# A first transpose copy moved from ScalarE to VectorE, and a pair's queries placed ahead of an exponential

## The chip, the cores and the metric

The kernel runs on one core of one Trainium2 chip. The core has five engines that run their own instruction streams and meet at semaphores: TensorE (PE, matmuls and transposes into PSUM), VectorE (DVE), ScalarE (ACT), GpSimd (POOL) and SyncE (SP). The metric is the device time of one execution in microseconds. A profile's span runs from the first to the last instruction, and the execution's own time is a little longer.

## The reference

Attention that selects chunks of keys, followed by a feed-forward network. Shapes: 4 batches, 8 heads, 768 tokens, 64 elements per head; the feed-forward goes from 512 to 2048 and back.

```python
k_min, k_max = min and max of k over chunks of 32 keys
ub = sum(maximum(q * k_min, q * k_max), axis=-1)      # one bound per query and chunk
ub = where(causal, ub, -1e9)
top_chunks = argsort(ub)[..., -6:]                    # six chunks per query
scores = where(selected & causal, q @ k.T / 8, -1e9)
attn = softmax(scores)
x = (attn @ v), heads side by side                    # 3072 x 512
h = maximum(x @ w_in, 0)
out = (h * h) @ w_out
```

## The kernel before

**Tiling.** A slot is one pair of heads in one half (384 tokens) of one batch. There are 32 slots, four to a half. `ORDER` gives the halves; slots 0 to 3 are the first half of batch 0, slots 4 to 7 the first half of batch 1. In the code a slot is `s`, `NP` is 4, and the fifth and sixth pairs are slots 4 (`s == NP`) and 5 (`s + 1`). All of it lies in one program without loops on the chip: the Python loops write the instruction order out by hand, and each engine works through its own list in that order.

**Steps of a slot.** `step_T` (L274) transposes keys and queries on PE into two PSUM tiles, `tk` and `tq`. `relus_T` (L295) makes ReLU of the queries and of their negatives on ACT (`qr`), which the bounds need. `extrema` (L237, L240) reduces the keys to minima and maxima per chunk on DVE (`km`, `kbd`). `place` (L300) copies transposed keys or queries, one head at a time, into the tile `kq` that the score matmuls read. `step_U` (L378 to L398) computes the bounds `ub` on PE, the sixth largest by MAX8 on DVE, and writes `chosen`. `step_V` transposes `chosen` on PE (`qt`, L442) and copies it on DVE under the queries in `kq` (L447), two copies. `step_E` (L460, L471) does the score matmuls of one head into a PSUM bank `ps` and the exponential on ACT into `e`. `step_F` (L493 to L503) multiplies with the values into `po`; DVE takes a reciprocal `r` and writes the normalised `x`.

**From x to the feed-forward.** For the first half, x is transposed on PE: `x_T` (L531) for slots 0 and 1 together into one PSUM tile `pt`, and again for slots 2 and 3. `x_copy` (L537) copies each `pt` into `xT`, 128 x 768 each. `push` then queues the feed-forward's blocks. `ffn_up` (L579) makes 128 of the 2048 inner columns with four matmuls, one for each head pair of `xT`, into `ph`; ACT applies the ReLU and DVE squares it. The first two blocks go straight to `h` (L585) and are squared later (L586); most others go over `ht` (L589, L590). `ffn_down` (L602) multiplies with `w_out`.

**PSUM tiles that are shared.** The pool `psF` has two banks under the tag `ph`. They are used in turn by `tk` of the early slots, the two `pt` tiles, and the `ph` blocks. The pool `psY` has one bank, which holds `tq` of the early slots one after the other: the sixth pair's `tq` waits until the fifth pair's queries have been placed.

**The order around the change.** Slot 3 is the last turn of the first loop. Its last turn does the exponentials of slot 3, `x_T(0, 0, F)`, its copy on ACT, the placing of the fifth pair's queries and of one head of its keys on ACT, `step_F(3)`, and `step_V(4)`. The next loop starts with slot 4: `step_P(5)` (the transposes of the sixth pair), `x_T(0, 1, F)` with its copy on DVE, `relus_T(5)`, the first exponential of slot 4 (`step_E(4, 0, 0)`), `push(0)`, and then `extrema(5)` and the placing of the sixth pair. The instructions of `push` are given out later by `f1()`, one block at a time.

**Loads.** POOL issues the loads of k, q, v and of both weights from lists by slot (`later`); `w_in` comes in three pieces (L631), `w_out` in two (L636). SP issues DMA transposes and the output. An issue on POOL waits until the one that used its semaphore eight issues before has landed.

Of the kernel before, what the change touches and what calls it, by code (L numbers as in the profile page):

```python
# [39 lines left out]
def kernel(  # L40
# [9 lines left out]
    nc = tc.nc  # L50
# [178 lines left out]
    def extrema(s, part=None):  # L229
        b, half, p = slots[s]  # L230
        kv = st[s]["k"].rearrange("r (j c e) -> r c j e", j=TP, c=12)
        if part in (None, 0):
            st[s]["km"] = work.tile([128, 2, 12], BF16, tag="km", name="km")
        km = st[s]["km"]
        for w in range(2):
            if part in (None, w):
                nc.vector.tensor_reduce(km[:, w, :], kv, axis=AX.XY, op=(ALU.min, ALU.max)[w])  # L237
        if part in (0, 1):
            return
        nc.vector.tensor_mul(  # L240
            kbds[b % 2][:, p, :, :, 12 * half:12 * half + 12], hmask,
            km.unsqueeze(2).to_broadcast([128, 2, 2, 12]))

    def in_order(x):

        return x.rearrange("r (j p) -> r p j", j=TP)

    def by_token(x):
        return x.rearrange("r (p j) -> r p j", j=TP)
# [36 lines left out]
    def relus_T(s):  # L286
        b, half, p = slots[s]
        t = st[s]
        qr = t["qr"] = work.tile([128, 2, HB], BF16, tag="qr", bufs=3, name="qr")
        c = 128 * (1 - half)  # L290
        for w in range(2):
            o, i = qr[:, w, c:], t["q"][:, c:]
            if s >= NP:
                o, i = by_token(o), in_order(t["q"])[:, c // TP:, :]
            nc.scalar.activation(o, i, ACT.Relu, scale=(-1.0, 1.0)[w])  # L295

    def place(s, n, copy, h0=0, h1=2):
        b, half, p = slots[s]
        for h in range(h0, h1):
            copy(by_token(kqs[b % 2][0:D, p, 2 * half + "kq".index(n), h, :]),  # L300
                 in_order(st[s][n][D * h:D * h + D]))
# [216 lines left out]
    def xT_of(hb):  # L518
        if hb not in xTs:
            xTs[hb] = late.tile([128, NKI, HB], BF16, tag="xT", name="xT")  # L520
        return xTs[hb]
# [14 lines left out]
    def x_copy(hb, g, u0, u1, copy):  # L536
        copy(xT_of(hb)[:, 2 * g + u0:2 * g + u1, :], pts[hb, g][:, u0:u1, :])  # L537
# [143 lines left out]
    def busy(n, pool=psA, tag="att"):  # L681

        idle = pool.tile([128, 128], F32, tag=tag, name="idle")
        for _ in range(n):
            nc.tensor.matmul(idle, lhsT=ident, rhs=ident, start=True, stop=True)  # L685
# [33 lines left out]
    for s in range(NP):  # L719
        last = s + 1 == NP  # L720
        if s:
            step_E(s, 0, 0)
            if not last:

                step_T(s + 2, F, Y, "k")
                extrema(s + 2, 0)
            step_E(s, 0, 1)
        if last:
            step_F(s - 1, 0)
            step_F(s - 1, 1)  # L730
        step_E(s, 1, 0)
        step_U(s + 1)
        if not last:
            busy(3)
            extrema(s + 2, 1)
            place(s + 1, "k", nc.scalar.copy)
        step_E(s, 1, 1)
        if last:
            x_T(0, 0, F)
            x_copy(0, 0, 0, 2, nc.scalar.copy)  # L740
            place(s + 1, "q", nc.scalar.copy)
            place(s + 1, "k", nc.scalar.copy, 1, 2)
            step_F(s, 0)
            step_F(s, 1)
            step_V(s + 1)
        else:
            step_T(s + 2, F, Y, "q")
            relus_T(s + 2)
            step_V(s + 1)
            if s:  # L750
                step_F(s - 1, 0)
                step_F(s - 1, 1)
            extrema(s + 2, 2)
            if s + 2 == NP:
                place(s + 2, "k", nc.vector.tensor_copy, 0, 1)
        go(s, 99)
# [6 lines left out]
    for s, (b, half, p) in enumerate(slots):  # L763
        if s < NP:
            continue
        hb = s // NP
        nb = len(BANKS[half])
        hf = nb // 2
        quota = [((5, 5, 4, 4) if hb == 1 else (8, 5, 6, 7) if hb == 2 else (8, 6, 7, 7))[p]]
        for fn, *a in first.get(s, ()):  # L770
            fn(*a)
        if (hb == ON_PE - 1 and p == 2) or (ON_PE < hb < 2 * B - 1 and p == 0):
            parts.extend(step_K(hb + 1))

        def f1():
            if quota[0] and queue:
                quota[0] -= 1
                fill(1, True)

        if s == NP:  # L780
            step_P(s + 1)
            x_T(0, 1, F)
            x_copy(0, 1, 0, 2, nc.vector.tensor_copy)
            relus_T(s + 1)
            for n in range(hf):
                step_E(s, 0, n)
            push(0)
            extrema(s + 1)
            place(s + 1, "k", nc.vector.tensor_copy)
            place(s + 1, "q", nc.scalar.copy)  # L790
        if s == 2 * NP:
            for n in range(hf):
                step_E(s, 0, n)
            relus_T(s + 1)
            place(s + 1, "q", nc.scalar.copy)
            step_F(s - 1, 0)
            step_F(s - 1, 1)
            f1()
            x_T(1, 1, F, (1,))
            f1()  # L800
            extrema(s + 1)
            place(s + 1, "k", nc.vector.tensor_copy)
            put_off()
            x_copy(1, 1, 1, 2, nc.vector.tensor_copy)
            push(1)
        if p == 0 and hb > 2:
            step_F(s - 1, 0)
            step_F(s - 1, 1)
            put_off()
            push(hb - 1)  # L810
        else:
            f1()
        if s > NP and s != 2 * NP:
            for n in range(hf):
                step_E(s, 0, n)
        k1()
        f1()
        if p == 0 and hb > 2:
            f1()
            f1()  # L820
        if hb > 1 and s != 2 * NP:
            f1()
        if hb < ON_PE:
            go(s, 4 if s == 2 * NP else 2)
        for n in range(hf, nb):
            step_E(s, 0, n)
        if hb < ON_PE and p:
            k1()
        if s + 1 == ON_PE * NP:
            f1()  # L830
        if s < NS - 2 or s + 1 == 3 * NP:
            step_U(s + (1 if hb < ON_PE else 2))
        if s == NP:
            put_off()
        if s + 1 == ON_PE * NP:
            put_off(2)
        if hb >= ON_PE and s < NS - 2:
            step_W(s + 2)
        if s == 2 * NP:

            for x in nsel:
                nc.vector.memset(
                    x[:, :, :, :, 1, :].rearrange("p i h j c -> p (i h j) c"), 0.0)
        late_f = half == 0 and hb > 2
        border = p == 0 and hb > 1
        if not border and not (late_f and p == NP - 1) and s + 1 not in (2 * NP, 3 * NP):
            f1()
        if p and s > NP:
            step_F(s - 1, 0)
            step_F(s - 1, 1)  # L850
        for fn, *a in by_sp.get(s, ()):
            fn(*a)
        if s + 1 == ON_PE * NP:
            step_P(s + 2)
            step_Q(s + 2)
        if half == 0 and not (late_f and p in (0, NP - 1)):
            f1()
        if hb < ON_PE and p:
            k1()
        for n in range(hf):  # L860
            step_E(s, 1, n)
            if border and half and n == 0:

                f1()
        if not (late_f and p == 0):
            f1()
        if s + 1 <= ON_PE * NP:
            step_V(s + 1)
        if s + 1 == ON_PE * NP:
            put_off(2)  # L870
        if hb == ON_PE and p == 0:
            parts.extend(step_K(hb + 1))
        k1()
        if hb < ON_PE:
            go(s, 99)
        for n in range(hf, nb):
            step_E(s, 1, n)
        if hb >= ON_PE:
            go(s, 99)
        k1()  # L880
        if hb == ON_PE - 1 or (hb == ON_PE and p):
            k1()
        if s + 1 < ON_PE * NP:
            step_P(s + 2)
            if s + 2 == ON_PE * NP:
                step_Q(s + 2)
        if s + 1 == ON_PE * NP:
            f1()
            step_U(s + 2)
            step_W(s + 2)  # L890
        if hb >= ON_PE or s + 1 == ON_PE * NP:
            if s + 3 < NS:
                step_P(s + 3)
                step_Q(s + 3)
        f1()
        if half == 0:
            f1()
        while quota[0] and queue:
            f1()
# [40 lines left out]
```

## Time and profile before

| | |
|---|---|
| median of 3 runs | 265.12 us (264.89 to 265.48) |
| profiled execution, its own time | 265.17 us |
| its span | 263.5 us |
| granted TensorE clock | 1.00 |
| PE busy | 253.6 us (96%) |
| ACT busy | 178.4 us (68%) |
| DVE busy | 162.9 us (62%) |
| POOL busy | 91.0 us (35%) |

A row of a timeline gives the start, the time it took, the engine, the line, the operation, and out<-in with shapes; "x6" merges six instructions in a row. In brackets stands the idle time of the engine just before, and what ended it. A row of the chain gives start, length and what. PEld is PE's weight load, and L12 is line 12 of the kernel before. Matmul ends are modelled, and successors on ACT and DVE may start a little before their predecessor's recorded end.

### The profile page before, as it was taken

How to read it: one execution, taken by the hardware profiler on the slowest of the kernel's cores; microseconds unless marked ns; L12 is line 12 of the kernel's file. 1: busy time of each engine (PE TensorE's matmuls, PEld its weight loads, DVE VectorE, ACT ScalarE, POOL GpSimd, SP SyncE). 2: the span in 40 equal slices, each digit the busy share in tenths (PEclk: the TensorE clock that was granted, in tenths of full speed). 3: DMA queues.
4: the chain of work that ended last, by engine and by line, in shares of the span. 5: the costliest groups of instructions: out<-in, count | busy, mean ns of one | idle time of the engine just before them, and what ended most of it. 6: DMA issues, size and time to landing. Idle time of an engine off the chain costs nothing.

```text
span 263.5 us, 6549 instructions
## 1 busy us (share of the span) xinstructions
PE 253.6 (96%) x2398; PEld 157.4 (60%) x2424; DVE 162.9 (62%) x619; ACT 178.4 (68%) x399; POOL 91.0 (35%) x134
## 2 busy tenths in 40 slices
PE   7898899999999999999999999999999999999995
PEld 6576565556676566655565566745565665645543
DVE  6788998867995568566875566554863233424411
ACT  4899997698984787944785778835685788614500
POOL 8957445607911444225520552310221111000000
PEclk9999999999999999999999999999999999999999
DMA  7999999999994999999995999995642220111022
GB/s 138 166 188 188 207 219 183 131 196 137 135 154 96 138 163 165 142 152 150 189 133 138 142 145 145 166 165 131 112 110 62 67 45 17 56 42 41 0 82 80
DMA packets 116162, 33.69 MB, mean 128 GB/s; under 512 B 102561, under 2 KB 112577, under 8 KB 116129
## 3 DMA queue, kind: packets, MB, share of 16 engines
q0 software_dynamic: 65200, 13.83, 64.0%
q1 hardware_dynamic: 49984, 19.03, 38.2%
q10 hardware_dynamic: 944, 0.39, 0.6%
q8 instruction: 19, 0.31, 0.5%
q14 instruction: 15, 0.11, 0.2%
HBM read 27.26 MB, written 6.29 MB: 127 GB/s over the span
## 4 chain that ended last, share of the span: by engine, by line
PE 88%; ACT 5%; DVE 4%; issue 2%; POOL 0%; ACTq 0%; POOLq 0%
PE ph L579 29%; PE py L602 29%; PE ps L460 13%; PE po L493 8%; ACT e L471 2%; PE ub L382 2%; PE idle L685 2%; PE py L567 1%; PE tk L274 1%; ACT kq L300 1%; DVE km L343 1%; PE qt L431 1%; DVE km L237 1%; PE qt L442 1%; ACT qr L295 1%
## 5 line engine op out<-in xcount | busy, mean ns | idle before, releaser
L471 ACT ACTIVATE e<-ps 128x512 bf16<-128x512 f32 x192 | 96.8, 550 | 18.6 <-PE ps L460 16.9
L579 PE MATMUL ph<-xT,w_in 128*128 128x384 bf16 x512 | 98.9, 325 | 0.7 <-ACT h L585 0.5
L602 PE MATMUL py<-w_out,h 128*128 128x512 bf16 x342 | 82.7, 379 | 1.9 <-issue 0.3
L590 DVE TENSOR_TENSOR h<-ht 128x384 bf16<-128x384 bf16 x114 | 41.8, 376 | 55.4 <-ACT ht L589 54.9
L475 POOL TENSOR_SCALAR_AFFINE_SELECT e<-e 128x384 bf16<-128x384 bf16 x56 | 30.1, 537 | 127.6 <-ACT e L471 127.5
L589 ACT ACTIVATE ht<-ph 128x384 bf16<-128x384 f32 x114 | 55.5, 500 | 26.9 <-PE ph L579 26.5
L579 PEld LDWEIGHTS <-w_in 128*128 128x128 bf16 x512 | 47.9, 97 | 31.4 <-issue 2.1
L460 PE MATMUL ps<-kq 96*128 96x384 bf16 (+2 forms) x320 | 58.0, 278 | 1.4 <-DVE kq L436 1.2
L602 PEld LDWEIGHTS <-h 128*128 128x128 bf16 x368 | 34.7, 97 | 35.3 <-issue 0.6
L460 PEld LDWEIGHTS <-kq 96*128 96x128 bf16 x320 | 26.4, 97 | 16.1 <-issue 1.7
L493 PEld LDWEIGHTS <-e 128*128 128x128 bf16 x672 | 25.2, 98 | 3.9
L493 PE MATMUL po<-vn,e 128*128 128x65 bf16 x672 | 26.8, 194 | 0.0
L396 DVE MAX8 m<-ub 128x8 f32<-128x16 f32 (+4 forms) x160 | 16.2, 168 | 15.7 <-PE ub L389 9.3
L608 ACT COPY ob<-py 128x512 f32<-128x512 f32 x18 | 10.6, 586 | 22.6 <-PE py L602 22.3
L503 DVE TENSOR_TENSOR x<-po,r 128x384 bf16<-128x384 f32 x32 | 17.8, 558 | 1.1
L109 POOL DMA_DIRECT2D kn<-in_k_dram x15 | 13.4, 897 | 0.4 <-issue 0.3
L237 DVE TENSOR_REDUCE km<-tk 128x12 bf16<-128x384 bf16 x24 | 12.5, 551 | 1.5 <-PE tk L274 1.2
L109 POOL DMA_DIRECT2D qn<-in_q_dram x15 | 13.3, 895 | 0.2
L125 POOL DMA_DIRECT2D vn<-in_v_dram x15 | 12.5, 842 | 2.3 <-DMA qn<-in_q_dram 1.5
L343 DVE TENSOR_TENSOR km<-km 128x384 bf16<-128x384 bf16 (+3 forms) x40 | 12.0, 300 | 1.1
L382 PEld LDWEIGHTS <-qr 128*128 128x128 bf16 x160 | 7.8, 96 | 4.1 <-DVE qr L323 1.0
L382 PE MATMUL ub<-kbd,qr 128*128 128x48 bf16 (+1 forms) x160 | 9.6, 180 | 0.6 <-DVE kbd L240 0.3
(79 smaller groups left out, 193.3 us busy)
## 6 DMA issues: line engine op xcount, KB each, us to landing
out_dram<-ob SPq DMA_DIRECT2D x23, 256.0 KB, 2.5
w_out<-in_moe_w_out_dram POOLq DMA_DIRECT2D x2, 1024.0 KB, 18.0
kn<-in_k_dram POOLq DMA_DIRECT2D x15, 128.0 KB, 6.0
qn<-in_q_dram POOLq DMA_DIRECT2D x15, 128.0 KB, 5.8
kq<-kqT SPq DMA_DIRECT2D x10, 192.0 KB, 4.7
vn<-in_v_dram POOLq DMA_DIRECT2D x4, 384.0 KB, 8.1
vn<-in_v_dram POOLq DMA_DIRECT2D x9, 128.0 KB, 8.0
w_in<-in_moe_w_in_dram POOLq DMA_DIRECT2D x2, 512.0 KB, 9.2
```

Of the source, the lines that this page charges most:

```text
L109: nc.gpsimd.dma_start(out=nat_of(n, g)[:, DM * j:DM * j + DM].rearrange("p (h d) -> p h d", d=D), in_=rows(n, *ORDER[g], 0, H)[:, 128 * j: ...
L382: nc.tensor.matmul(ub[:, j - j0], lhsT=st[s]["qr"][:, w, 128 * j:128 * (j + 1)], rhs=kbds[b % 2][:, p, w, :, 0:ncs], start=bool(half) and ...
L396: nc.vector.max(out=m8[:, j, hh, :], in_=ub[:, j - j0, hh, 0:12 * half + 4 * j + 4])
L460: nc.tensor.matmul(ps[:, at:at + 128 * m], lhsT=kqs[b % 2][0:KR, p, 2 * (j // HT), hh, 128 * (j % HT):128 * (j % HT + 1)], rhs=qc(s, hh)[: ...
L471: nc.scalar.activation(e[:, 512 * n + lo:512 * n + hi], ps[:, lo:hi], ACT.Exp, scale=float(scale))
L475: nc.gpsimd.affine_select(out=d, in_=d, compare_op=ALU.is_ge, fill=0.0, base=0, channel_multiplier=-1, pattern=[[0, 3], [1, 128]])
L493: nc.tensor.matmul(po[:, hh, i, :], lhsT=t["e"][hh][:, c:c + 128], rhs=vn[b % 2][:, 2 * p + hh, j, :], start=(j == 0), stop=(j == iq))
L503: nc.vector.tensor_mul(x[:, p].rearrange("p j (h d) -> p h j d", h=2), po[:, :, :, 0:D], r.to_broadcast([128, 2, HT, D]))
L579: nc.tensor.matmul(ph[:, 0:HB], lhsT=w_in[:, ki, 128 * f:128 * (f + 1)], rhs=xT[:, ki, :], start=(ki == 0), stop=(ki == NKI - 1))
L589: nc.scalar.activation(ht, ph[:, 0:HB], ACT.Relu)
L590: nc.vector.tensor_mul(h, ht, ht)
L602: nc.tensor.matmul(py[t], lhsT=h2[hb, f][:, 128 * t:128 * (t + 1)], rhs=w_out[:, f, :], start=(f == 0), stop=(f == NFI - 1))
```

## The change

Two lines. The copy of the first `pt` (slots 0 and 1) into `xT` is written by `nc.vector.tensor_copy` instead of `nc.scalar.copy`. It keeps its place in the program: on DVE it stands between the selection (`chosen`) of the fifth pair and the reciprocal of slot 3. And the placing of the sixth pair's queries (two copies on ACT) is called ahead of `step_E(4, 0, 0)` instead of behind the placing of its keys. On ACT these copies then stand between the ReLUs of the sixth pair and the fifth pair's first exponential. The orders of PE, POOL and SP are the same as before.

```diff
@@ -737,7 +737,7 @@
         step_E(s, 1, 1)
         if last:
             x_T(0, 0, F)
-            x_copy(0, 0, 0, 2, nc.scalar.copy)
+            x_copy(0, 0, 0, 2, nc.vector.tensor_copy)
             place(s + 1, "q", nc.scalar.copy)
             place(s + 1, "k", nc.scalar.copy, 1, 2)
             step_F(s, 0)
@@ -782,12 +782,12 @@
             x_T(0, 1, F)
             x_copy(0, 1, 0, 2, nc.vector.tensor_copy)
             relus_T(s + 1)
+            place(s + 1, "q", nc.scalar.copy)
             for n in range(hf):
                 step_E(s, 0, n)
             push(0)
             extrema(s + 1)
             place(s + 1, "k", nc.vector.tensor_copy)
-            place(s + 1, "q", nc.scalar.copy)
```

## The prediction

> **What bounds the kernel now.** I read the page's head and chain first, then the busy time by stage, then the chain and the rows of each engine around 20 to 30 us, where the changed lines run.
>
> ```profile
> span 263.5 us, 6549 instructions
> PE 253.6 (96%) x2398; PEld 157.4 (60%) x2424; DVE 162.9 (62%) x619; ACT 178.4 (68%) x399; POOL 91.0 (35%) x134
> PE 88%; ACT 5%; DVE 4%; issue 2%; POOL 0%; ACTq 0%; POOLq 0%
> ```
>
> TensorE (PE) is the bound over the whole span: busy 253.6 of 263.5 us, and 88% of the chain that ended last. The next rows give busy time in stretches of the span (length, then busy time and count of each engine, then clock, DMA share and GB/s).
>
> ```profile
> 24.00:28.00 4.00, 3.31 (x29) 2.06 (x26) 3.53 (x12) 3.35 (x9) 2.21 (x4) 1.00 1.47 202
> ...
> 30.00:38.00 8.00, 7.68 (x85) 4.91 (x81) 7.63 (x26) 7.32 (x20) 4.13 (x7) 1.00 1.28 215
> ...
> 60.00:120.00 60.00, 59.38 (x613) 37.73 (x617) 43.32 (x173) 43.99 (x97) 25.95 (x35) 1.00 1.33 145
> 120.00:180.00 60.00, 59.38 (x525) 36.21 (x531) 36.23 (x149) 40.39 (x88) 21.41 (x30) 1.00 1.31 149
> ```
>
> From 60 to 180 us PE has about 1% idle, at a granted clock of 1.00, so a lead won before that should last. In 24 to 28 us PE is busy only 3.31 of 4 us. There the chain (start, length, what) runs through ScalarE (ACT):
>
> ```profile
> 21.89 0.69 ACT xT L537
> ...
> 23.88 0.66 ACT qr L295 x2
> ...
> 24.56 0.35 issue
> 24.91 0.60 ACT e L471
> ...
> 26.38 0.50 ACT h L585
> ...
> 26.92 1.46 PE ph L579 x8
> ...
> 30.20 0.28 DVE kq L447
> ```
>
> The reader is to see that the copy to be moved stands in this chain, that 0.35 us ahead of the fifth pair's first exponential have no cause the profile names, and that the next feed-forward matmuls start 0.04 us behind the first ReLU (26.38 + 0.50).
>
> **The change part by part.** First the copy of x's first two transposes. ACT's own rows:
>
> ```profile
> 21.77 0.81 ACT L537 COPY xT<-pt 128x768 bf16<-128x768 bf16 x1
> 22.45 0.97 ACT L300 COPY kq<-tq 64x384 bf16<-64x384 bf16 x2
> 23.32 0.47 ACT L300 COPY kq<-tk 64x384 bf16<-64x384 bf16 x1
> ...
> 25.41 0.95 ACT L300 COPY kq<-tq 64x384 bf16<-64x384 bf16 x2
> ```
>
> ACT loses one instruction, and the fifth pair's query copies start at 21.77 instead of 22.45: 0.68 us earlier. What waits for them on PE:
>
> ```profile
> 21.05 0.50 PE L531 MATMUL pt<-ident,x 128*128 128x128 bf16 x6
> ...
> 23.47 0.37 PE L274 MATMUL tq<-ident,qn 96*64 96x96 bf16 x8 [0.80 <-ACT kq L300]
> 23.77 0.51 PE L531 MATMUL pt<-ident,x 128*128 128x128 bf16 x6
> 24.12 0.38 PE L460 MATMUL ps<-kq 96*128 96x384 bf16 x2
> ...
> 24.99 1.14 PE L579 MATMUL ph<-xT,w_in 128*128 128x384 bf16 x6 [0.16 <-DVE xT L537]
> ...
> 26.14 0.25 PE L382 MATMUL ub<-kbd,qr 128*128 128x24 bf16 x4
> 26.92 1.30 PE L579 MATMUL ph<-xT,w_in 128*128 128x384 bf16 x7 [0.53 <-ACT h L585]
> ```
>
> The sixth pair's query transposes (tq) share one bank with the fifth pair's and sat 0.80 us on those copies. They move from 23.47 to 22.79, and ACT's two ReLUs behind them (qr) from 23.88 to 23.20, ending 23.86: 0.68 us of the chain.
>
> VectorE (DVE) gains one instruction. Its rows:
>
> ```profile
> 21.77 0.21 DVE L398 TENSOR_TENSOR chosen<-ub,m 128x48 bf16<-128x48 f32 x1
> 22.28 0.20 DVE L502 RECIPROCAL r<-po 128x6 f32<-128x6 f32 x1 [0.30 <-PE po L493]
> 22.51 0.56 DVE L503 TENSOR_TENSOR x<-po,r 128x384 bf16<-128x384 f32 x1
> 23.10 0.60 DVE L447 COPY kq<-qt 32x256 bf16<-32x256 bf16 x2
> 24.38 0.56 DVE L537 COPY xT<-pt 128x768 bf16<-128x768 bf16 x1 [0.68 <-ACT qr L295]
> 24.85 1.01 DVE L237 TENSOR_REDUCE km<-tk 128x12 bf16<-128x384 bf16 x2
> ...
> 28.78 0.61 DVE L590 TENSOR_TENSOR h<-ht 128x384 bf16<-128x384 bf16 x2
> 29.81 0.36 DVE L590 TENSOR_TENSOR h<-ht 128x384 bf16<-128x384 bf16 x1 [0.42 <-ACT ht L589]
> ```
>
> The price of the added copy is in the row of its twin, 128x768 at 24.38: 0.56 us, and the next instruction starts 0.47 us after it. Its transposes end at 21.55 (21.05 + 0.50). DVE is free between 21.89 and 21.98 (successors overlap by about 0.1 us), so I put the copy at 21.89 and the reciprocal at 22.36 instead of 22.28. The idle 0.30 us ahead of the reciprocal covers the copy but for 0.08 us; without that cover it would cost 0.47. Queued behind it on DVE are the normalisation of x, then to end at 23.15 instead of 23.07, and the two code copies, at 23.18. The fifth pair's scores and the second set of x's transposes wait for these.
>
> The second set of transposes needs that x, and the tq ahead of it on PE (done 22.79 + 0.30). So it moves from 23.77 to 23.18, not to 23.09: late next is x, by DVE, and the lead there is 0.59 us. The second copy on DVE follows from 24.38 to 23.79, and the feed-forward's wait for it (24.99) to 24.40. The reductions and everything behind them on DVE take the same 0.59; if the copy starts at 21.98, 0.50.
>
> [...]
>
> Second, the order on ACT. The two copies of the sixth pair's queries (0.95 together) now go ahead of the exponential. No instruction is added, no DMA is issued, and PE's, POOL's and SP's orders are unchanged. The copies need only tq, ready since 23.16. They start about 23.76 (an ACT successor starts 0.10 us before its predecessor's recorded end: 24.91 + 0.60 against 25.41) and end at 24.71. The exponential's scores on PE move with x from 24.12 to 23.53 and end by 23.91, so they are there. It starts at 24.61, which is still before 24.91.
>
> What the 0.35 us of unnamed wait does is not shown by the trace. Its bounds are nothing (it was something that now passes under the copies) and 0.35 again (it belongs to this instruction). A cost above 0.35 has no row. I take nothing, because the copies put 0.7 us between the scores' end and the exponential, and I keep 0.35 for the range.
>
> The sum at the first ReLU of the feed-forward: 24.61 + 0.50 = 25.11 instead of 26.38, or 25.46 with the 0.35 us. Its matmuls are done by 24.9 (24.40 + 0.49 for two). It ends at 25.61 and the next matmuls could start at 25.65. PE itself is then just through the bound's matmuls (ub), which wait for DVE: 26.14 - 0.59 = 25.55, plus about 0.15. So they start at 25.70 instead of 26.92, a lead of 1.2 us; with the 0.35 us at 26.00, a lead of 0.9.
>
> Late next is DVE. It runs without a gap from 24.38 to 29.39 and carries 0.59; then comes the idle 0.42 ahead of the product at 29.81, which waited for ACT's ht. ACT and PE are 0.9 to 1.2 us earlier there, so the product can move by 0.59 + 0.42 = 1.01 us. From 30.20, in the stretch 30 to 38, DVE (7.63 of 8) paces the loop and hands its lead on. The lead is then the smaller of DVE's 1.01 and PE's 1.2 (or 0.9): 1.0, or 0.9.
>
> The profiled execution took 265.17 us by its own time, 1.67 more than its span, and 0.05 above the median of 265.12. 265.17 - 1.0 is 264.17, or about 264.15 as a median.
>
> **The rivals.** The lead of 1.0 us must pass the weights that are still loading:
>
> ```profile
> 20.41 0.77 POOL L631 DMA_DIRECT2D w_in<-in_moe_w_in_dram  x1
> ...
> 22.49 0.93 POOL L636 DMA_DIRECT2D w_out<-in_moe_w_out_dram  x1
> ...
> 32.29 0.67 POOL L104 DMA_DIRECT2D qn<-in_q_dram  x1 [0.94 <-DMA w_in<-in_moe_w_in_dram]
> ```
> ```profile
> 33.31 0.81 PE L579 MATMUL ph<-xT,w_in 128*128 128x384 bf16 x4
> ```
>
> *Most of the lead is taken back.* The last half of w_in, issued at 20.41, was in by 32.29, when POOL's wait for it ended. The ninth up-projection block, the first to read it, ran at 33.31 and would now be ready at 32.3. There is no room left: a landing 0.5 us later, or a product wait that doesn't give up its 0.42, leaves 0.5 to 0.6 us of lead, a time of about 264.65. Against it: in this execution the landing still fits, and DVE's loop at 30 to 38 had the block's matmuls well ahead of their use.
>
> *The copy holds up DVE, and the kernel is slower.* POOL writes DMA issues from 20.41 to 23.42 (22.49 + 0.93) without a stop. If DVE's copy can't run beside them, it starts at 23.42 instead of 21.89. Each 0.1 us of delay takes 0.1 from the 0.59, so nothing is left at 22.48; the 0.42 of idle covers to 22.90; from there the kernel is slower. At 23.42 it loses 0.5 us: 265.7. Against it: the normalisation at 22.51 also reads PSUM, ran beside the w_out issue, and took 0.56 us. [...]
>
> *The reorder does nothing by itself.* If PE had been ready later than ACT, placing the queries first would only delay the exponential. The rows say otherwise (0.53 us of PE idle on the ReLU). With the copy's move alone DVE's 0.59 would be the lead, near the first rival's time.
>
> **How the numbers follow.** The forecast (lead 0.9 to 1.0, 264.1 to 264.3) has 0.67. Most of the lead taken back or not used (264.65) has 0.18; the copy held up (265.7) has 0.08. What I have not named has 0.07, spread as 0.03 faster, 0.02 same, 0.02 slower. A measurement of this kernel can tell about 0.2%, 0.53 us, from no change: the runs before spread from 264.89 to 265.48. Faster by more than that is below 264.59: 0.67 + 0.03 = 0.70. Within: 0.18 + 0.02 = 0.20. Slower: 0.08 + 0.02 = 0.10. The range goes from PE's full lead of 1.2 and 0.2 of spread (263.7) to the first rival with 0.36 of spread above it (265.0), which leaves out the held-up copy and part of the unnamed. The signs are not balanced, so there is no second range.
>
> **What would show it.** In the profile after: tq at about 22.8; a DVE copy of xT at 21.9 taking 0.56, with x's last normalisation less than 0.2 us later than before; the exponential behind the query copies at 24.6 without a gap; the feed-forward's third block near 25.7 to 26.0 and PE's 0.53 us of idle gone; the DVE product's 0.42 us of idle gone and the code copies of 30.20 near 29.2. The prediction is wrong if the copy starts after 22.5, if the 0.35 us comes back larger, if PE waits for w_in near 32.3, or if the lead seen at 30 us is not in the span.

## The result, and the profile after

The changed kernel takes 264.07 us (median of 6 runs, 263.95 to 264.68) against 265.31 us before (6 runs, 264.89 to 265.48): a ratio of 0.996, with a 95% interval of 0.9947 to 0.9973. The forecast was 264.15 us, within 263.7 to 265.0.

The profiled execution was the slowest of the six: 264.68 us by its own time. Its page's head and the chain's shares, and then busy time by stage (the stretch and its length, busy time and count of PE, PEld, DVE, ACT and POOL):

```profile
span 263.0 us, 6549 instructions
PE 254.2 (97%) x2398; PEld 157.9 (60%) x2424; DVE 163.2 (62%) x620; ACT 177.7 (68%) x398; POOL 91.0 (35%) x134
...
PE 86%; DVE 8%; ACT 3%; issue 2%; POOL 0%; DVEq 0%; ACTq 0%; POOLq 0%
```
```profile
24.00:28.00 4.00, 3.80 (x30) 2.29 (x29) 3.87 (x14) 3.58 (x9) 2.35 (x4) 1.00 1.43 205
...
30.00:38.00 8.00, 7.68 (x83) 4.95 (x81) 7.68 (x26) 7.43 (x20) 4.09 (x6) 1.00 1.29 214
```

PE is busy 3.80 of 4 us in 24 to 28, where it was 3.31. VectorE's share of the chain has grown from 4% to 8%, ScalarE's fallen from 5% to 3%.

Two profiles of this kernel can't be laid over each other as they are: they start out of step. The second pair's normalisation of x, far ahead of the change, stands at 19.63 us before and at 19.95 after, from DVE's timelines:

```profile
19.63 0.56 DVE L503 TENSOR_TENSOR x<-po,r 128x384 bf16<-128x384 f32 x1
```
```profile
19.95 0.56 DVE L503 TENSOR_TENSOR x<-po,r 128x384 bf16<-128x384 f32 x1
...
22.10 0.21 DVE L398 TENSOR_TENSOR chosen<-ub,m 128x48 bf16<-128x48 f32 x1
22.37 0.56 DVE L537 COPY xT<-pt 128x768 bf16<-128x768 bf16 x1
22.84 0.19 DVE L502 RECIPROCAL r<-po 128x6 f32<-128x6 f32 x1
23.07 0.56 DVE L503 TENSOR_TENSOR x<-po,r 128x384 bf16<-128x384 f32 x1
...
24.28 0.56 DVE L537 COPY xT<-pt 128x768 bf16<-128x768 bf16 x1
24.76 1.01 DVE L237 TENSOR_REDUCE km<-tk 128x12 bf16<-128x384 bf16 x2
25.80 0.18 DVE L240 TENSOR_TENSOR kbd<-hmask,km 128x48 bf16<-128x48 bf16 x1
...
28.45 0.94 DVE L590 TENSOR_TENSOR h<-ht 128x384 bf16<-128x384 bf16 x3
29.43 0.60 DVE L447 COPY kq<-qt 32x256 bf16<-32x256 bf16 x2
```

So every time after is 0.32 us late for reasons that lie ahead of the change, and a lead is counted from that row in each profile. The code copies at 30.20 before stand at 29.43: 0.77 earlier as printed, 1.09 us with the 0.32. ACT's and PE's rows of after:

```profile
22.09 0.95 ACT L300 COPY kq<-tq 64x384 bf16<-64x384 bf16 x2
...
23.50 0.66 ACT L295 ACTIVATE qr<-tq 128x256 bf16<-128x256 bf16 x2
24.05 0.95 ACT L300 COPY kq<-tq 64x384 bf16<-64x384 bf16 x2
25.02 0.60 ACT L471 ACTIVATE e<-ps 128x512 bf16<-128x512 f32 x1
25.52 1.04 ACT L585 ACTIVATE h<-ph 128x384 bf16<-128x384 f32 x2
```
```profile
23.09 0.37 PE L274 MATMUL tq<-ident,qn 96*64 96x96 bf16 x8
23.47 0.55 PE L531 MATMUL pt<-ident,x 128*128 128x128 bf16 x6
...
26.04 0.25 PE L382 MATMUL ub<-kbd,qr 128*128 128x24 bf16 x4
26.14 1.46 PE L579 MATMUL ph<-xT,w_in 128*128 128x384 bf16 x8
```

ACT has no gap left ahead of the exponential, PE none ahead of the third feed-forward block, which now follows the bound's matmuls (ub) at once.

### The profile page after: what moved, and what is told of

The parts are those of the page before. It is cut to its first block, busy times and chain, and to the rows that moved or that the text cites. A ratio compares the mean times of both kernels' runs of the same rounds, so it can differ in the third digit from the quotient of the medians.

```text
span 263.0 us, 6549 instructions
## 1 busy us (share of the span) xinstructions
PE 254.2 (97%) x2398; PEld 157.9 (60%) x2424; DVE 163.2 (62%) x620; ACT 177.7 (68%) x398; POOL 91.0 (35%) x134
## 4 chain that ended last, share of the span: by engine, by line
PE 86%; DVE 8%; ACT 3%; issue 2%; POOL 0%; DVEq 0%; ACTq 0%; POOLq 0%
PE py L602 29%; PE ph L579 28%; PE ps L460 12%; PE po L493 7%; PE idle L685 2%; PE ub L382 2%; DVE km L343 2%; ACT e L471 1%; PE py L567 1%; PE qt L431 1%; PE tk L274 1%; DVE kq L436 1%; DVE x L503 1%; DVE km L237 1%; DVE kq L447 1%
## 5 line engine op out<-in xcount | busy, mean ns | idle before, releaser
L608 ACT COPY ob<-py 128x512 f32<-128x512 f32 x18 | 10.5, 586 | 22.6 <-PE py L602 22.3
L503 DVE TENSOR_TENSOR x<-po,r 128x384 bf16<-128x384 f32 x32 | 17.8, 558 | 1.1
```

The lines of the kernel that those rows point to most:

```text
L503: nc.vector.tensor_mul(x[:, p].rearrange("p j (h d) -> p h j d", h=2), po[:, :, :, 0:D], r.to_broadcast([128, 2, HT, D]))
```

## The experiments

Each is a small edit. For each I give the time, and from its profile the lead over the kernel before at two rows of DVE's L503, counted from the second pair's normalisation: at the fifth pair's (before: 34.70 - 19.63 = 15.07 us) and at the eighth pair's (47.77 - 19.63 = 28.14), and at the end of the span (263.5 - 19.63 = 243.9). A positive lead is earlier. The second column is the time of that second pair's row.

| kernel | second pair at | lead at fifth pair | at eighth pair | at the end | median, runs |
|---|---|---|---|---|---|
| changed | 19.95 | 1.09 | 1.08 | 0.8 | 264.07, 6 |
| copy only | 19.18 | 0.77 | 0.77 | 0.9 | 264.44, 7 |
| order only | 19.46 | 0.49 | 0.48 | 0.5 | 264.68, 11 |
| touched early | 19.67 | 0.98 | 0.27 | 0.3 | 264.57, 11 |
| copy behind codes | 19.43 | 0.86 | 0.85 | 0.9 | 264.20, 8 |
| no first mask | 19.63 | 0.94 | 1.05 | 1.1 | 264.14, 5 |
| copy twice | 19.31 | 0.51 | 0.50 | 0.6 | 264.47, 11 |
| w_in in halves | 19.66 | 0.96 | 0.88 | 0.9 | 264.45, 12 |
| w_in in halves, again | 19.27 | -0.06 | -0.29 | -0.3 | 264.76, 12 |
| squares late | 19.45 | 1.01 | -0.13 | -0.1 | 264.84, 8 |
| changed again | 19.32 | 0.95 | 1.07 | 0.9 | 264.30, 5 |

The kernel before had 265.04 us (26 runs) beside the first four, 264.96 (30 runs) beside the next four and 265.34 (12 runs) beside the last two.

A lead in the table is that of one execution. Two kernels were profiled twice: the changed one (1.09 and 0.95 at the fifth pair) and the one with w_in in halves (0.96 and -0.06). So a small difference between two leads shows something only where the rows behind it are seen.

**The copy alone and the order alone.**

```diff
-            x_copy(0, 0, 0, 2, nc.scalar.copy)
+            x_copy(0, 0, 0, 2, nc.vector.tensor_copy)
```

> The copy on VectorE, the sixth pair's queries in their old place behind the first exponential and the feed-forward's first blocks' call. Theory A (two parts that add up: 0.68 us of ScalarE from the copy, the rest from the unnamed 0.35 us ahead of the exponential passing under the query copies): 0.7 to 0.8 us faster than before, 264.5, and the gap ahead of the exponential is still there. Theory B (VectorE alone sets the end of the lead, the order on ScalarE is hidden): as fast as the whole change, 264.1, whatever the gap does.

```diff
             relus_T(s + 1)
+            place(s + 1, "q", nc.scalar.copy)
             for n in range(hf):
...
             place(s + 1, "k", nc.vector.tensor_copy)
-            place(s + 1, "q", nc.scalar.copy)
```

> The copy stays on ScalarE, the sixth pair's queries ahead of the exponential. Theory A: the gap of 0.35 us is gone, the ReLU at 26.38 comes 0.4 us earlier, and VectorE's idle 0.42 us gives as much: 0.4 us faster than before, 264.9. Theory B: without VectorE's own lead the order brings nothing that lasts: 265.3, as before.

Ratios to before: 0.9976 (0.9966 to 0.9987) and 0.9987 (0.9978 to 0.9996). ACT's exponential in the copy alone, then in the order alone, from their timelines:

```profile
23.69 0.60 ACT L471 ACTIVATE e<-ps 128x512 bf16<-128x512 f32 x1 [0.30 <-PE ps L460]
```
```profile
24.25 0.95 ACT L300 COPY kq<-tq 64x384 bf16<-64x384 bf16 x2
25.23 0.60 ACT L471 ACTIVATE e<-ps 128x512 bf16<-128x512 f32 x1
```

Theory A holds: each part gives its own lead, 0.77 and 0.49 us, and together 1.09, a little less than their sum. In the medians the parts give 0.60 and 0.36 us. Theory B does not fit the copy alone. Its second copy of x comes as early as in the changed kernel (23.51 - 19.18 and 24.28 - 19.95, both 4.33 us), but then a product on DVE waits for ACT, and the code copies stand at 28.98 - 19.18 = 9.80 us instead of 29.43 - 19.95 = 9.48:

```profile
28.59 0.36 DVE L590 TENSOR_TENSOR h<-ht 128x384 bf16<-128x384 bf16 x1 [0.26 <-ACT ht L589]
```

With the copy alone the gap ahead of the exponential stands (0.30), and there the profile names the scores' matmuls; with the order alone it is gone. What the 0.35 us of before were is not settled: the scores had ended at 24.50 there by their modelled end, 0.4 us ahead of the exponential; in the copy alone it started 0.09 us behind them (23.22 + 0.38, 23.69).

**One copy, two places, two times.** First the waits of the copy are met earlier, by a write of one column two slots ahead:

```diff
         last = s + 1 == NP
+        if s == 2:
+            nc.vector.memset(xT_of(0)[:, 0, 0:1], 0.0)
```

> The changed kernel, with one column of xT set to zero by VectorE two slots earlier, so that the six waits of the first copy (four DMA queues, ScalarE, TensorE) are mostly met there and the copy itself waits for TensorE alone. Theory: the 0.2 us between the selection and the copy in the profile of after are the sequencer's work on these waits, and lie on the path: the copy starts 0.2 us earlier and the time falls by 0.1 to 0.2 us, 263.9. Rival: those pieces pass beside the selection's own run-out, and nothing moves: 264.1. If the early write costs VectorE the same 0.2 us on the path of its own slot, the time is also 264.1, but the copy's wait pieces are gone.

The chain of after (DVEq is VectorE's sequencer), and DVE's timeline of this kernel:

```profile
22.10 0.04 DVE chosen L398
22.13 0.05 issue
22.18 0.05 DVEq L537
...
22.37 0.56 DVE xT L537
```
```profile
21.81 0.21 DVE L398 TENSOR_TENSOR chosen<-ub,m 128x48 bf16<-128x48 f32 x1
21.94 0.55 DVE L537 COPY xT<-pt 128x768 bf16<-128x768 bf16 x1
```

The pieces are real: the copy starts 0.27 us after the selection in after and 0.13 here, and x comes 0.17 earlier counted from the second pair. The trace of after has three semaphore instructions for this copy (22.1 to 22.3 us, 0.02 to 0.05 us each); that the waits are six, no trace shows. They did not come over from ACT. In before, ACT's copy had one of its own, and the three stood at 22.5 to 22.7 ahead of VectorE's second copy, which waited longer for its transposes anyway. They go with the first copy into xT on VectorE.

But nothing is won: the time is 264.57 us (ratio 0.9979, 0.9969 to 0.999). By the code copies the 0.17 us are gone already (29.26 - 19.67 = 9.59 us, against 9.48 in after), since a square and a product were held beside POOL's work on the way (more on this below). Then the profile shows another wait, on PE and on POOL:

```profile
33.06 0.82 PE L579 MATMUL ph<-xT,w_in 128*128 128x384 bf16 x4 [0.61 <-DMA w_in<-in_moe_w_in_dram]
```
```profile
33.30 0.67 POOL L104 DMA_DIRECT2D qn<-in_q_dram  x1 [3.04 <-DMA w_in<-in_moe_w_in_dram]
```

The ninth block waited 0.61 us for the last half of w_in, and the lead fell from 0.98 to 0.27. This is the prediction's first rival, in a kernel where it wasn't looked for. In after the same POOL row stands at 32.16 and the block ran at 32.54 without a wait. Why w_in landed later here is not shown. The profiled execution (264.94 us) was slower than the median of its kernel, so the wait need not be in every run.

Then the copy goes behind x and the code copies:

```diff
-            x_copy(0, 0, 0, 2, nc.vector.tensor_copy)
             place(s + 1, "q", nc.scalar.copy)
...
             step_V(s + 1)
+            x_copy(0, 0, 0, 2, nc.vector.tensor_copy)
```

> The changed kernel with the first copy behind the third pair's normalisation and the code copies on VectorE, right ahead of the second copy. Theory: the copy's 0.47 us lie on VectorE's path either way, since VectorE runs without a gap from the selection to the second copy; x and the second transposes come 0.5 us earlier, the second copy does not: within 0.2 us of the changed kernel, 264.0 to 264.3. Rival: x's lateness (0.24 us in the profile of after against before) holds the second transposes and so the end: 0.2 to 0.3 us faster than the changed kernel.

264.20 us, 0.9968 (0.9957 to 0.9979): within the spread of the changed kernel. x comes as early as before the change (22.31 - 19.43 = 2.88 us after the second pair, as 22.51 - 19.63), and that wins nothing. VectorE's work is not the same as expected, though: the idle time ahead of the reciprocal is back, which the copy covered in part in its first place.

```profile
22.08 0.20 DVE L502 RECIPROCAL r<-po 128x6 f32<-128x6 f32 x1 [0.30 <-PE po L493]
...
23.54 1.02 DVE L537 COPY xT<-pt 128x768 bf16<-128x768 bf16 x2
```

The second copy ends 24.56 - 19.43 = 5.13 us after the second pair, 0.24 later than in after (24.28 + 0.56 - 19.95 = 4.89), and the lead is 0.86 instead of 1.09. The medians are too coarse to show it.

And the copy made twice in a row, which computes the same:

```diff
             x_copy(0, 0, 0, 2, nc.vector.tensor_copy)
+            x_copy(0, 0, 0, 2, nc.vector.tensor_copy)
```

> The changed kernel with the first copy made twice in a row on VectorE. Theory: with the change, VectorE runs without idle time from the selection to the code copies at 29.4 us, so every 0.47 us added there takes 0.47 from the lead: 0.4 to 0.5 us slower than the changed kernel, 264.5. Rival: TensorE's and ScalarE's lead sets the end and VectorE has room: 0 to 0.15 us slower.

264.47 us, 0.998 (0.9971 to 0.9989). The second transposes stop for x (PE's timeline), and the lead falls from 1.09 to 0.51:

```profile
23.63 0.34 PE L531 MATMUL pt<-ident,x 128*128 128x128 bf16 x3 [0.47 <-DVE x L503]
```

So VectorE has no room up to the second copy: 0.59 us of added copy take 0.58 of lead. From there the delay goes on over PE and ACT, not over VectorE's own list. PE's blocks wait for the second copy (24.84 - 19.31 = 5.53 us, against 24.90 - 19.95 = 4.95), and VectorE's last product then waits 0.29 us for ACT's ht (28.98). The exponential also shows the unnamed gap again, 0.42 us behind the modelled end of its scores (23.94 + 0.38), though the queries stand ahead of it:

```profile
24.74 0.60 ACT L471 ACTIVATE e<-ps 128x512 bf16<-128x512 f32 x1 [0.39 <-ACT kq L300]
```

So the new order doesn't remove that wait. In the changed kernel it passes under the query copies.

**The masking beside VectorE.**

```diff
-        if n == 1 and s >= NP:
+        if n == 1 and s >= NP and (s, hh) != (NP, 0):
             d = e[:, 0:1152].rearrange("p (a c) -> p a c", a=3)[:, :, 0:128]
             nc.gpsimd.affine_select(
```

> The changed kernel without the causal masking of the first head of the fifth pair (one affine_select on GpSimd left out; the rest is computed). Theory: a VectorE operation with two inputs in SBUF that meets this masking is held by it (0.67 us instead of 0.35 in the profile of after, 0.90 in that of before); without it the two squares and the three products behind them take 0.35 each, the code copies come 0.1 to 0.3 us earlier counted from the second pair's normalisation, then held by TensorE or ScalarE; the time is 0 to 0.2 us less than the changed kernel's. Rival: the long operation has another cause, stays long without the masking, and the time is the changed kernel's.

In the profile of before the first square of a feed-forward block took 0.90 us, beside a masking on POOL; in after the second took 0.67. From the timelines: DVE's row and POOL's of before, the same two of after, then DVE's squares and products without the masking:

```profile
27.69 0.90 DVE L586 TENSOR_TENSOR h<-h 128x384 bf16<-128x384 bf16 x1
```
```profile
27.82 0.54 POOL L475 TENSOR_SCALAR_AFFINE_SELECT e<-e 128x384 bf16<-128x384 bf16 x1
```
```profile
27.86 0.67 DVE L586 TENSOR_TENSOR h<-h 128x384 bf16<-128x384 bf16 x1
```
```profile
27.69 0.63 POOL L475 TENSOR_SCALAR_AFFINE_SELECT e<-e 128x384 bf16<-128x384 bf16 x1
```
```profile
27.27 0.61 DVE L586 TENSOR_TENSOR h<-h 128x384 bf16<-128x384 bf16 x2
27.81 0.62 DVE L590 TENSOR_TENSOR h<-ht 128x384 bf16<-128x384 bf16 x2
28.71 0.36 DVE L590 TENSOR_TENSOR h<-ht 128x384 bf16<-128x384 bf16 x1 [0.29 <-ACT ht L589]
```

The held operations end 0.23 and 0.21 us after the masking does (27.82 + 0.54 and 27.69 + 0.63). Without it two squares take 0.61 together. The time, 264.14 us (0.9957, 0.9942 to 0.9972), is the changed kernel's: VectorE then waits 0.29 us for ACT's ht, and the code copies come at 29.11 - 19.63 = 9.48 us after the second pair, as in after (29.43 - 19.95).

**w_in's last half in two DMAs**, run twice:

```diff
-    at(1, load_w_in, 1024, 2048)
+    at(1, load_w_in, 1024, 1536)
+    at(1, load_w_in, 1536, 2048)
```

> The changed kernel with the last half of w_in loaded by two DMAs of 512 columns instead of one of 1024. Theory: the ninth up-projection block then waits for a landing near 29 us instead of 32 to 33 us; in the run with the early write TensorE stood 0.6 us on it, and in some runs of the changed kernel it must have, so slow runs of it fall away: median 263.9 and a narrower spread. Rival: in the changed kernel the landing always fits, and one more issue on GpSimd (0.77 us) in a full queue delays w_out or the next keys: 264.1 to 264.4.

> The early write to xT (which took the wait pieces off the copy) and w_in's last half in two DMAs together. Theory: the early write alone lost what it won to w_in; with w_in in time it keeps its lead of about 1.0 us at the fifth pair's normalisation: 263.9 to 264.1, against 264.6 for the early write alone. Rival: the early write costs VectorE as much as the copy saves and the loss is not w_in's: 264.4 to 264.6.

The second kernel does not have the early write that its expectation names: its text is the first one's line by line, its trace has no early write to xT, and its copy starts 0.27 us after the selection (21.41, 21.68), not 0.13. So the two edits together were not run, and neither the theory nor the rival of that expectation is tested. What the two runs show is one kernel twice.

It doesn't help: 264.45 us (0.9978, 0.9968 to 0.9988) and 264.76 (0.9989, 0.9978 to 1.0), 12 runs each. The 0.31 us between them are a measure of what two medians of one kernel can differ by. PE no longer waits for w_in in either profile, but the additional issue comes ahead of the maskings on POOL, and these then follow one another. In the second profile a product on DVE was held for both of them (DVE's row, then POOL's):

```profile
28.35 1.20 DVE L590 TENSOR_TENSOR h<-ht 128x384 bf16<-128x384 bf16 x1
```
```profile
27.41 0.91 POOL L636 DMA_DIRECT2D w_out<-in_moe_w_out_dram  x1
28.32 1.01 POOL L475 TENSOR_SCALAR_AFFINE_SELECT e<-e 128x384 bf16<-128x384 bf16 x2
```

It ended at 29.55, 0.22 us behind the second masking (28.32 + 1.01), and the whole lead at the fifth pair is gone. In the first profile the last product started at 28.74, just ahead of the maskings at 28.80, took 0.36 us, and the code copies stood at 29.13 - 19.66 = 9.47 us, as in after. So whether a product is held there decides over most of the lead, and it differs between executions of one kernel.

**The squares later**, as an attempt at a faster version, and the changed kernel once more beside it:

```diff
-        if s == NP:
-            put_off()
...
+        if s == NP + 3:
+            put_off(2)
         if s > NP and s != 2 * NP:
```

> The changed kernel with the squares of the feed-forward's first two blocks (two VectorE operations, 0.27 us each start to start, more where they meet a masking) taken out of the stretch near 27.5 us and put at the start of the eighth pair, near 43 us, ahead of the first use of those blocks. Theory: VectorE sets the lead from 24 to 42 us, so the code copies and all behind them come earlier, as far as TensorE and ScalarE allow (their lead is 1.2 us against VectorE's 1.09): 0.1 to 0.3 us faster than the changed kernel at the end, if the squares find room at 43 us. Rival: ScalarE's and TensorE's order already holds the products, or TensorE waits for the late squares ahead of its first down-projection: no faster, up to 0.4 us slower than the changed kernel.

> The changed kernel once more, beside the one with the late squares, for a direct comparison and a second profile of it: 264.0 to 264.3. In its profile the lead at the second normalisation of x behind the change, counted from the second pair's normalisation, is 1.1 us again, whatever the start of the run was; the loss of 0.28 us at 70 to 75 us of the first profile returns only if the same VectorE operations meet GpSimd's again.

264.84 us (0.998, 0.9969 to 0.9991) against 264.30 (0.9961, 0.9948 to 0.9973). The rival was right twice. With the squares gone the products wait for ACT, and the code copies come no earlier (28.92 - 19.45 = 9.47 us). And PE's first down-projection stops; the page names ACT, which had long been done, while VectorE's two late squares ran from 42.89 to 43.50, the first until about 43.24:

```profile
43.29 1.09 PE L602 MATMUL py<-w_out,h 128*128 128x512 bf16 x3 [0.60 <-ACT h L585]
```

Before that, 0.21 us of its lead were lost from the fifth to the sixth pair (34.70 to 40.17 in before, 33.51 to 39.19 here): the ninth block ran at 32.31, 0.28 us later behind the matmuls ahead of it than in after, and 0.24 us ahead of POOL's row that had waited for w_in (32.55), as in the kernel with the early write (33.06, 33.30). So w_in held it here too, by the rows. No version here beats the changed kernel.

## Why the prediction was right, by its steps

Times of after are given less 0.32 us.

- *tq at 22.79.* Measured 22.77. The 0.68 us of ACT were the copy, and the copy alone gave 0.77 in the end.
- *The copy on DVE at 21.89, 0.56 us long, x 0.08 late.* It took 0.56, but started at 22.05, and x was 0.24 late. The term was too small by the sequencer's work on the copy's waits, which the early write took away again (0.27 to 0.13). "Less than 0.2 us later" was wrong by little.
- *VectorE's lead 0.59 at the second copy.* 24.28 - 0.32 against 24.38: 0.42.
- *The exponential at 24.61 without a gap, the ReLU at 25.11.* 24.70 and 25.20. Taking nothing for the 0.35 us was right here, and for the reason given, that the copies cover it: with later scores, in the kernel with the copy made twice, the gap came back as 0.39.
- *The third block at 25.70, a lead of 1.2.* 25.82, a lead of 1.10. The order was as told: the bound's matmuls start 0.06 us behind the end of VectorE's kbd (25.80 + 0.18, 26.04), and the block comes right behind. PE's own queue reaches them at the same time, and the profile lists no idle time there; both hang on the second copy.
- *VectorE's 0.59 + 0.42 of idle = 1.01, and the smaller of the two leads.* The idle time is gone and the code copies lead by 1.09. The sum was right by its terms only in part: 0.42, 0.42 of idle, and some 0.23 because the squares to the first product took 1.09 us before (27.69 to 28.78) and 0.86 after (27.59 to 28.45), the masking holding them less. So two errors cancelled: the lead at the second copy was 0.17 smaller than forecast, and the maskings gave 0.23 that the sum didn't have. That part of the agreement is luck. VectorE's lead and that of ACT and PE came out equal, as the runs without the masking and with late squares show, so each limit alone would have given about the same.
- *The lead lasts.* Up to 65 us it does. In both profiles of the changed kernel some 0.3 us are lost at 70 to 75 us, at VectorE operations beside a masking, and from there to the end the lead stays at 0.8 to 0.9. In the medians it is 1.24 us in the first comparison and 1.04 in the last, against 0.97 by the forecast (265.12 to 264.15). That the time itself came out within 0.08 us of the forecast is luck in part, since the median before was 265.31 this time. That the loss occurs in every run isn't shown; the copy alone and the order alone have none.
- *The rivals.* The copy was not held up behind POOL's issues: it took 0.56 us (from 22.37 as printed) beside that of w_out (22.15 to 23.10), the same as its twin in before. The reorder did something by itself (0.49). PE did not wait for w_in in the changed kernel's two profiles. In two other kernels it did, and there the block ran 0.24 us ahead of POOL's row that waited for w_in; in the second profile of the changed kernel it ran 0.03 us behind that row (31.91, 31.88), so I estimate 0.27 us of room. That is little, if not none as the prediction said; how often the changed kernel meets the wait is not shown.

## What to carry to other kernels

Where a chain alternates between two engines, take the work off the one that the waits end on only as far as the other has idle time in the same stretch, and look which row ends up next: here both limits met at 1.1 us, and neither more nor less work on one side helped. Count the start of each profile first: compare from a row ahead of the change, not from zero. Look at the semaphore instructions ahead of a moved instruction too: here the first copy into xT on VectorE carried three. Before the change they passed under a wait, and the move put them on the path: the copy started 0.27 us after the selection, and 0.13 us after it with the early write.

## What the runs showed of the hardware

**In these profiles some squares and products on VectorE were held beside a masking on GpSimd.** A square or product of 128x384, with both inputs in SBUF, took 0.35 us alone; those shown above that were held beside one or two maskings took 0.67 to 1.20 and ended 0.21 to 0.23 us after them. The prediction asked whether the copy would be held, which reads PSUM and took 0.56 us, and not whether the squares would. They were also held beside a DMA issue of POOL with no masking running: in the kernel with the early write the first of two squares took 0.68 us beside w_out's issue (DVE's row has both, then POOL's row). In the two profiles of w_in in halves a product took 0.67 and 0.70 there. In the kernel without the masking, two squares that started later in the issue took 0.35 each, so what part of an issue holds them is open. Nor do the recorded starts tell who is held: the square of before started 0.13 us ahead of the masking (27.69, 27.82), the product in the first profile of w_in in halves 0.06 us ahead, and only the square was held.

```profile
27.15 0.95 DVE L586 TENSOR_TENSOR h<-h 128x384 bf16<-128x384 bf16 x2
```
```profile
27.01 0.90 POOL L636 DMA_DIRECT2D w_out<-in_moe_w_out_dram  x1 [0.72 <-DMA vn<-in_v_dram]
```

The place at 70 us, DVE's row and POOL's of before and then of after, from the timelines:

```profile
70.95 0.73 DVE L343 TENSOR_TENSOR km<-km 128x96 bf16<-128x96 bf16 x2
```
```profile
70.87 0.52 POOL L475 TENSOR_SCALAR_AFFINE_SELECT e<-e 128x384 bf16<-128x384 bf16 x1
```
```profile
70.12 1.15 DVE L343 TENSOR_TENSOR km<-km 128x96 bf16<-128x96 bf16 x2
```
```profile
70.61 0.59 POOL L475 TENSOR_SCALAR_AFFINE_SELECT e<-e 128x384 bf16<-128x384 bf16 x1
```

**The start differs from run to run, and PE's rate in it.** Ten warming matmuls near 5.9 us, before and after, which nothing in the change touches:

```profile
5.90 0.73 PE L685 MATMUL idle<-ident 128*128 128x128 bf16 x10
```
```profile
5.90 1.25 PE L685 MATMUL idle<-ident 128*128 128x128 bf16 x10
```

In after these ran at about half the rate, one started every 0.10 us instead of every 0.06, though the granted clock stands at 1.00 in both, and the 0.32 us begin here. The ten took 0.73 us in nine of the twelve profiles, and 0.81, 0.98 and 1.25 us in the others. The second pair's normalisation lay between 19.18 and 19.95 us over all profiles. Between the two profiles of the changed kernel it differs by 0.63 us, which is nearly all of the 0.7 us between their spans (263.0 and 262.3). What sets PE's rate there is not shown.
